# A retention chunk as one step, and the first down stage of a fused RetNet and SwiGLU kernel laid out anew

## The chip, the cores and the metric

The kernel runs on one core of a Trainium2 chip. The metric is the device time of one execution in microseconds (us), the median of three runs. The core's engines are TensorE (PE, matmuls; PEld is its weight load), VectorE (DVE), ScalarE (ACT), GpSimd (POOL) and SyncE (SP), which here only issues DMAs. Each engine has a queue of its own; ACT also issues the stores of the output.

## The reference

A retention layer (a linear recurrence with a decay for each head) is followed by a SwiGLU feed-forward block:

```python
batch, n_heads, seq, head_dim = (4, 8, 768, 64)       # q, k, v
n_tokens, d_model, d_ff = (3072, 512, 1536)           # the block behind it

gamma = 1.0 - 2.0 ** (-5.0 - np.arange(H, dtype=np.float32))
for t in range(S):
    state = gamma[None, :, None, None] * state + np.einsum('bhd,bhe->bhde', k[:, :, t], v[:, :, t])
    y[:, :, t] = scale * np.einsum('bhd,bhde->bhe', q[:, :, t], state)

g = x @ w_gate                       # x: y as (3072, 512)
silu = g * (1.0 / (1.0 + np.exp(-g)))
val = x @ w_val
return (silu * val @ w_out).astype(np.float32)
```

## The kernel before

All arithmetic is fp32. The 3072 tokens are worked through in four segments (s = 0 to 3), each of two halves of three blocks of 128 tokens. A segment has an **up stage** (x by gate and value weights, giving hT) and a **down stage** (hT by w_out). While the down stage of segment s runs, the retention of segment s+1 is done beside it.

Big products use a Strassen scheme in Winograd's form: 7 block products in place of 8, paid for with additions of operands on DVE. The first segment's up stage uses one level. The later ones (`up2`) use two levels: 21 *units* of weights, each of 7 sub-products. A unit's four inner blocks lie in DRAM (`unit_b`, written in the first segment). The three sums that make it whole are done once on DVE (`sums_u`), and the finished unit is stored (`unit_t`), so that the later segments only load it. Some units are summed in the first down stage (`to_sum`), the rest inside the second segment's up stage, two stages ahead of their use. A unit is loaded to one of six ring buffers of which the first four serve the sums in the first down stage.

```python
def load_unit(n, whole, slot=None):
    t = ring[n % RING if slot is None else slot]
    ...
    if whole:
        nc.sync.dma_start(out=t, in_=unit_t[n])                 # 896 KB
    else:
        nc.sync.dma_start(out=t[:, :, ds(U11, 4)], in_=unit_b[n // 7][:, SLOT[PRODUCTS[n % 7]]])

def sums_u(n, engine=nc.vector):                                # three steps
    ...                       # L170: 128x512; L174 and L178: 128x256
    def last():
        sub(w[:, :, U4], w[:, :, U21], w[:, :, U2], op=ALU.subtract)
        nc.sync.dma_start(out=unit_t[n], in_=w)
```

Retention works by chunks of 128 tokens. A chunk has three parts on PE, with tiles of other shapes than the big products: scores (L385, 64x128 tiles; DVE multiplies the result by the decay mask, L391), y (`mix`: L442 with 64x64 and L446 with 128x64 tiles; ACT copies it to xT) and the state (L424, 128x64; DVE adds it, L429). Before:

```python
def retention(s):
    cs = seg_chunks(s)                       # six chunks

    def first(n):
        scores(cs[n]); scale_k(cs[n]); scale_q(cs[n])

    def last(n):
        decay(cs[n]); state(cs[n])
        del chunks[cs[n]]
        if n + 3 < len(cs):
            load_chunk(cs[n + 3], places_of(n))

    steps = [lambda: first(0)]
    for n, c in enumerate(cs):
        if n + 1 < len(cs):
            steps.append(lambda n=n: first(n + 1))
        steps.append(lambda c=c: mix(c))
        steps.append(lambda n=n: last(n))
        if n % 2:
            steps.append(lambda n=n: sums_x(n // 2))
    return steps
```

The down stage handles its three token blocks u = 0, 1, 2 with seven products each (6 matmul steps of 128x256, two passes each in fp32, so 12 in the profile). `step()` is called after each product and puts other work there. `more` makes the next block's operand sums (`sum_h`), `second` is the product B21 and its addition (L727):

```python
if u == 0:
    first(0, range(2, FH)); first(1)
    if s == 0:
        sums_d(0); sum_h(1, 0); second(0); do("t4")      # t4, t5: two last states
        sum_h(2, 0); sums_d(1); second(1); do("t5")      # of the first segment
        sum_h(4, 0); sum_h(3, 0); sums_d(2)
elif u == 2:
    first(u)
product(wb, T1, cur[1]);  nc.scalar.copy(p5, wb);               step()
product(x, T2, cur[2], start=False);  nc.scalar.copy(u2, x);    step()
product(wb, B22, cur[4], start=False)
tt(ev[0][:, DH:], wb, u2, op=ALU.add);  more(1, 2, 4);          step()   # L768
product(x, T3, cur[3], start=False)
tt(ev[1][:, DH:], x, p5, op=ALU.add);  more(3);                 step()   # L772
if s or u == 2:
    second(u)
product(x, T4, a_dn(1, 1, u), start=False)
nc.scalar.copy(ev[1][:, :DH], x)                                         # L778
for i in range(2):
    nc.scalar.dma_start(out=out[ds(row, P)], in_=ev[i]);                 # L782
step()
```

In `up2`, a stage takes 7 time units (one unit is a sub-product of 4 matmuls), and every operation has its time in the list:

```python
at(base, product, x, U11, a[:, 0, 0], True)         # +2 U1, +4 U2, +6 U22, +8 U3, +10 U21, +12 U4
if old is None:
    at(base + 0.5, copy, c11, x);   at(base + 2.5, copy, c22, wb)        # ACT
    at(base + 4.5, copy, c12, x);   at(base + 12.5, copy, c21, x)
...
elif p == 3:   by_block(15.8, 14.3, lambda r: tt(h0[:, r], h0[:, r], p1[:, r], op=mul))   # L663
...
if n + RING < NU:
    at(base + 13.2, load_unit, n + RING, n + RING in prepared)
m = n + 2
if m < NU and m not in prepared:
    for when, k in ((2.2, 0), (4.8, 1), (6.8, 2)):
        at(base + when, lambda k=k: sums_u(m)[k]())
```

The main loop sets what is loaded, summed and stepped beside a down stage:

```python
resident = list(range(RING - 2))
to_sum = list(range(RING - 1, NU, 2)) + resident         # 5, 7, ... 19, then 0 to 3
...
steps = retention(s + 1) + [lambda ps=ps: sums_2(*ps) for ps in ((5, 6), (1, 2), (7,))]

def step():
    k = count[0] = count[0] + 1
    retain((k > 2) + (4 < k < 13) if s else (k > 5) + (7 < k < 18))      # so many steps
    ...
    if count[1] < len(to_sum) and count[1] * 15 < (k - 5) * len(to_sum):
        n = to_sum[count[1]]
        load_unit(n, False, n if n in resident else count[1] % (RING - 2))
        sums.extend(sums_u(n))
        count[1] += 1
    while sums and count[2] * 15 < (k - 6) * 3 * len(to_sum):
        sums.pop(0)()
        count[2] += 1

for u in range(L):
    down(s, u, step)
for st in steps + sums:
    st()
if nxt:
    sums_2(3); sums_2(4)
```

Of the kernel before, what the change touches and what calls it, by code (L numbers as in the profile page):

```python
# [16 lines left out]
P = 128  # L17
# [7 lines left out]
L = 3  # L25
# [16 lines left out]
def tile_retnet_swiglu(  # L42
# [336 lines left out]
    def scores(c):  # L379
        kt, qt = (pairs(t) for t in chunks[c][:2])  # L380
        sp = [bank("s") for i in range(2)]
        for n in range(NP):
            for i in range(2):
                r = ds(D * i, D)
                nc.tensor.matmul(sp[i][:, ts(n, P)], kt[r, n], qt[r, n],  # L385
                                 start=True, stop=True, skip_group_check=True)
        a = []
        for i in range(2):
            j = turn["a"] = turn.get("a", -1) + 1
            t = pairs((iop if c in first_chunks else midp)[:, ts(j % 4, 512)])  # L390
            nc.vector.tensor_tensor(t, pairs(sp[i]), mask[:, i], op=ALU.mult)  # L391
            a.append(t)
        att[c] = a


    def scale_q(c, engine=nc.gpsimd):
        if c % NCK:
            qt = pairs(chunks[c][1])
            engine.tensor_tensor(qt, qt, qdec, op=ALU.mult)

    def scale_k(c, engine=nc.gpsimd):
        if c % NCK < NCK - 1:
# [50 lines left out]
    def retention(s):  # L453

        cs = seg_chunks(s)

        def first(n):
            scores(cs[n])  # L460
            scale_k(cs[n])
            scale_q(cs[n])

        def last(n):
            decay(cs[n])
            state(cs[n])
            del chunks[cs[n]]
            if n + 3 < len(cs):
                load_chunk(cs[n + 3], places_of(n))

        steps = [lambda: first(0)]
        for n, c in enumerate(cs):
            if n + 1 < len(cs):
                steps.append(lambda n=n: first(n + 1))
            steps.append(lambda c=c: mix(c))
            steps.append(lambda n=n: last(n))
            if n % 2:
                steps.append(lambda n=n: sums_x(n // 2))
        return steps

# [219 lines left out]
    def down(s, u, step):  # L700


        x = banks[(u or 0) % 2][:, :DH]

        def product(o, slot, a, start=True):
            for k in range(FH):
                nc.tensor.matmul(o, a[:, k], wot[k][:, slot], start=(start and k == 0),  # L707
                                 stop=(k == FH - 1), skip_group_check=True)

        def tmp(i):  # L710
            return iop[:, ts(8 + i, DH)]

        def first(u, ks=range(FH)):
            o = banks[u % 2][:, :DH]
            for k in ks:
                nc.tensor.matmul(o, a_dn(0, 0, u)[:, k], wot[k][:, B11], start=(k == 0),  # L716
                                 stop=(k == FH - 1), skip_group_check=True)
# [12 lines left out]
        def more(*ns):  # L730
            for n in ns:
                if u + 1 < L:
                    sum_h(n, u + 1)

        if u is None:
            return first
        ev = [iop[:, ts(2 * (u % 2) + i, DM)] for i in range(2)]
        tt = nc.vector.tensor_tensor
        if u == 0:
            first(0, range(2, FH))  # L740
            first(1)
            if s == 0:

                sums_d(0)
                sum_h(1, 0)
                second(0)
                do("t4")
                sum_h(2, 0)
                sums_d(1)
                second(1)  # L750
                do("t5")
                sum_h(4, 0)
                sum_h(3, 0)
                sums_d(2)
        elif u == 2:
            first(u)
        cur = dict(hs)
        wb = bank("wz")[:, :DH]
        product(wb, T1, cur[1])
        p5 = tmp(2)  # L760
        nc.scalar.copy(p5, wb)
        step()
        product(x, T2, cur[2], start=False)
        u2 = tmp(3)
        nc.scalar.copy(u2, x)
        step()
        product(wb, B22, cur[4], start=False)
        tt(ev[0][:, DH:], wb, u2, op=ALU.add)  # L768
        more(1, 2, 4)
        step()  # L770
        product(x, T3, cur[3], start=False)
        tt(ev[1][:, DH:], x, p5, op=ALU.add)  # L772
        more(3)
        step()
        if s or u == 2:
            second(u)
        product(x, T4, a_dn(1, 1, u), start=False)
        nc.scalar.copy(ev[1][:, :DH], x)  # L778
        p, pos = divmod(s * L, NCK)
        for i in range(2):  # L780
            row = (2 * p + i) * S + (pos + u) * P
            nc.scalar.dma_start(out=out[ds(row, P)], in_=ev[i])  # L782
        step()


    kept_vk = consts.tile([P, 2, 512], F32, name="kept_vk")
# [42 lines left out]
        g4 s5 S0 g5 x1 m4 a1 q5 C0 U T0 b1 m5 x2 U D D  # L829
    """)  # L830

    def retain(k):
        for _ in range(k):
            if steps:
                steps.pop(0)()

    for f in range(NF - 1):
        up(f)
# [9 lines left out]

    resident = list(range(RING - 2))
    to_sum = list(range(RING - 1, NU, 2)) + resident
    prepared = set(to_sum)

    for s in range(NSEG):
        nxt = seg_chunks(s + 1) if s + 1 < NSEG else []
        if s == 0:
            for i in range(3):
                load_chunk(nxt[i], places_of(i))
        else:  # L860

            ends = [(7 * n + 13.4, lambda i=i: load_chunk(nxt[i], places_of(i)))
                    for i, n in ((0, NU - 5), (2, NU - 4), (1, NU - 3)) if nxt]


            def begin(s=s):
                down(s, None, None)(0, range(2))

            ends.append((7 * (NU - 1) + 11, begin))
            for n in range(RING - 2, RING):  # L870
                ends.append((-1, lambda n=n: load_unit(n, n in prepared)))
            up2(s, prepared, ends)
            prepared = set(range(NU))
        if s:
            for n in (1, 2, 4, 3):
                sum_h(n, 0)
        steps = []
        if nxt:
            att.clear()
            steps = retention(s + 1) + [lambda ps=ps: sums_2(*ps)  # L880
                                        for ps in ((5, 6), (1, 2), (7,))]
        count, sums = [0, 0, 0], []

        def step():

            k = count[0] = count[0] + 1
            retain((k > 2) + (4 < k < 13) if s else (k > 5) + (7 < k < 18))
            if not nxt:
                return
            if s:  # L890
                if k > 7 and k % 2 == 0 and k // 2 - 4 < RING - 2:
                    load_unit(k // 2 - 4, True)
                return
            if count[1] < len(to_sum) and count[1] * 15 < (k - 5) * len(to_sum):
                n = to_sum[count[1]]
                load_unit(n, False, n if n in resident else count[1] % (RING - 2))
                sums.extend(sums_u(n))
                count[1] += 1
            while sums and count[2] * 15 < (k - 6) * 3 * len(to_sum):
                sums.pop(0)()  # L900
                count[2] += 1

        for u in range(L):
            down(s, u, step)
        for st in steps + sums:
            st()
        if nxt:
            sums_2(3)
            sums_2(4)

# [48 lines left out]
```

## Time and profile before

| | us |
|---|---|
| time, median of 3 (lowest, highest) | 733.93 (733.56, 733.95) |
| span of the profiled execution | 732.1 |
| PE busy | 713.2 (97%) |
| DVE busy | 469.3 (64%) |
| ACT busy | 239.7 (33%) |
| POOL busy | 237.4 (32%) |

The granted TensorE clock is 1.00 throughout. By PE's timeline the first segment's retention runs to 29.3 us, its up stage to 146.5, the first down stage to 225.9; then the up stage of the second segment to 327.5, its down stage to 403.4, the third's to 501.0 and 577.6, the fourth's to 674.8 and the end. A line of the waits names the engine that waited and who released it. The timelines give start, duration and work; a block of several like instructions is one row. A row's duration on PE has the tail of its last matmul in it, so what a block costs is read from start to start.

### The profile page before, as it was taken

The numbers are of one execution on the slowest core, as the hardware profiler recorded it, in microseconds if no ns is written. First come the engines' busy times: TensorE is split into PE (matmuls) and PEld (weight loads), VectorE is DVE, ScalarE is ACT, GpSimd is POOL, SyncE is SP. The second block draws the span as 40 slices with busy tenths as digits, with TensorE's granted clock in tenths as the row PEclk, the third lists the DMA queues.
The fourth block names the chain that finished last, engine by engine and source line by source line (L and its number), as shares of the span: only waits on it lengthen the run. The fifth ranks groups of instructions, "written<-read, shape, count | busy, mean of one in ns | idle before, by whom it ended". The sixth has DMA issues, their size and how long they took to land.

```text
span 732.1 us, 11713 instructions
## 1 busy us (share of the span) xinstructions
PE 713.2 (97%) x4544; PEld 615.4 (84%) x4544; DVE 469.3 (64%) x836; ACT 239.7 (33%) x484; POOL 237.4 (32%) x147
## 2 busy tenths in 40 slices
PE   8898999999999999999999999999999999999997
PEld 7654555687789999998888999998888999999886
DVE  3888998676867888786355465657536356667420
ACT  2668777401212332421121333332121233233000
POOL 1333444512100728380300264363220063726000
PEclk9999999999999999999999999999999999999999
DMA  9797986705989767652642455560373065540010
GB/s 322 254 375 250 288 276 221 271 1 174 381 309 373 278 234 261 220 208 78 207 162 88 135 199 205 200 219 16 108 281 130 29 204 203 200 149 1 1 58 30
DMA packets 60824, 139.06 MB, mean 190 GB/s; under 512 B 4576, under 2 KB 27616, under 8 KB 60768
## 3 DMA queue, kind: packets, MB, share of 16 engines
q1 hardware_dynamic: 57312, 132.01, 52.5%
q10 hardware_dynamic: 3456, 6.29, 2.3%
q8 instruction: 36, 0.59, 0.3%
q14 instruction: 20, 0.16, 0.1%
HBM read 101.72 MB, written 36.57 MB: 189 GB/s over the span
## 4 chain that ended last, share of the span: by engine, by line
PE 85%; DVE 5%; DMA 3%; issue 2%; ACT 1%; SPq 0%; ACTq 0%; DVEq 0%
PE bank L624 37%; PE bank L707 24%; PE bank L513 13%; PE bank L716 4%; PE bank L385 3%; PE bank L446 2%; PE bank L442 2%; DMA ring<-unitb 2%; DMA hsp<-in_w_gate_dram 1%; PE bank L424 1%; DVE ring L170 0%; DVE iop L589 0%; DVE ring L289 0%; DVE midp L391 0%; DVE ring L178 0%
## 5 line engine op out<-in xcount | busy, mean ns | idle before, releaser
L624 PE MATMUL bank<-loadp,ring 128*128 128x192 f32 x720 | 140.6, 327 | 3.1 <-ACT midp L589 2.5
L707 PE MATMUL bank<-wot,hsp 128*128 128x256 f32 x576 | 131.7, 383 | 0.0
L624 PEld LDWEIGHTS bank<-loadp,ring 128*128 128x128 f32 x720 | 120.4, 190 | 4.8 <-ACT midp L589 3.6
L707 PEld LDWEIGHTS bank<-wot,hsp 128*128 128x128 f32 x576 | 107.5, 190 | 16.6 <-issue 1.0
L589 DVE TENSOR_TENSOR iop<-bank,iop 128x384 f32<-128x384 f32 x144 | 79.7, 555 | 56.2 <-PE bank L624 53.2
L624 PE MATMUL bank<-xs,ring 128*128 128x192 f32 x432 | 87.8, 326 | 0.0
L659 POOL TENSOR_TENSOR hT<-iop 128x768 f32<-128x768 f32 x36 | 66.5, 1847 | 36.7 <-DVE iop L589 36.7
L589 ACT COPY hsp<-bank 128x384 f32<-128x384 f32 x90 | 42.9, 479 | 100.4 <-PE bank L624 89.7
L589 POOL TENSOR_TENSOR iop<-hsp,midp 128x768 f32<-128x768 f32 x9 | 16.3, 1814 | 181.5 <-ACT hsp L589 181.5
L624 PEld LDWEIGHTS bank<-xs,ring 128*128 128x128 f32 x432 | 73.2, 190 | 0.0
L707 PE MATMUL bank<-wot,hT 128*128 128x256 f32 x288 | 66.2, 383 | 2.5 <-DVE iop L772 2.5
L624 PE MATMUL bank<-xT,ring 128*128 128x192 f32 x324 | 66.2, 327 | 1.1 <-DVE iop L589 1.1
L513 PE MATMUL bank<-xs,ring 128*128 128x384 f32 x192 | 64.7, 488 | 2.4 <-DVE xs L496 1.7
L707 PEld LDWEIGHTS bank<-wot,hT 128*128 128x128 f32 x288 | 53.8, 190 | 10.8 <-DVE iop L772 2.8
L513 PEld LDWEIGHTS bank<-xs,ring 128*128 128x128 f32 x192 | 36.1, 190 | 29.2 <-issue 2.3
L624 PE MATMUL bank<-hsp,ring 128*128 128x192 f32 x288 | 56.8, 327 | 0.0
L624 PEld LDWEIGHTS bank<-xT,ring 128*128 128x128 f32 x324 | 54.8, 190 | 2.3 <-DVE iop L589 2.2
L589 DVE TENSOR_TENSOR midp<-bank,midp 128x384 f32<-128x384 f32 x72 | 39.9, 555 | 22.8 <-PE bank L624 21.2
L513 PE MATMUL bank<-xT,ring 128*128 128x384 f32 x144 | 49.6, 488 | 1.6 <-DVE hT L550 1.6
L624 PEld LDWEIGHTS bank<-hsp,ring 128*128 128x128 f32 x288 | 48.3, 190 | 0.6 <-ACT hsp L589 0.6
L513 PEld LDWEIGHTS bank<-xT,ring 128*128 128x128 f32 x144 | 27.0, 190 | 21.3 <-DVE hT L550 2.2
L449 ACT COPY xT<-bank 128x512 f32<-128x512 f32 x24 | 14.1, 589 | 89.8 <-PE bank L446 89.8
(146 smaller groups left out, 966.3 us busy)
## 6 DMA issues: line engine op xcount, KB each, us to landing
ring<-unitt SPq DMA_DIRECT2D x50, 896.0 KB, 4.6
unitt<-ring SPq DMA_DIRECT2D x21, 896.0 KB, 4.7
unitb<-ring SPq DMA_DIRECT2D x12, 896.0 KB, 7.7
ring<-unitb SPq DMA_DIRECT2D x21, 512.0 KB, 6.4
out_dram<-iop ACTq DMA_DIRECT2D x24, 256.0 KB, 3.5
loadp<-in_w_val_dram SPq DMA_DIRECT2D x18, 256.0 KB, 3.9
loadp<-in_w_gate_dram SPq DMA_DIRECT2D x9, 512.0 KB, 6.4
midp<-in_w_out_dram SPq DMA_DIRECT2D x12, 256.0 KB, 6.1
```

The source lines that it names most:

```text
L385: nc.tensor.matmul(sp[i][:, ts(n, P)], kt[r, n], qt[r, n], start=True, stop=True, skip_group_check=True)
L424: nc.tensor.matmul(st[ds(D * i, D), n], kd[:, h], vn[:, h], start=(n == 0), stop=True, skip_group_check=True)
L442: nc.tensor.matmul(y[r, ts(n, P)], prev[r, n], qd[r, n], start=(n == 0), stop=False, skip_group_check=True)
L446: nc.tensor.matmul(y[ds(D * i, D), ts(n, P)], vn[:, ts(2 * n + i, D)], a[i][:, n], start=(ci == 0 and n == 0), stop=True, skip_group_check ...
L449: nc.scalar.copy(xT[:, :, c // NCK % 2, ts(ci % L, P)], pairs(y))
L513: nc.tensor.matmul(o, w[:, slot, k], a[:, k], start=(start and k == 0), stop=(stop and k == KH - 1), skip_group_check=True)
L589: events.append((t, len(events), lambda: fn(*args, **kw)))
L624: nc.tensor.matmul(o[:, h], w[:, h, slot], rhs, start=(start and h == 0), stop=True, skip_group_check=True)
L659: by_block(9.5, 13.5, lambda r: pool(to[:, r], u2[:, r], p5[:, r], op=add))
L707: nc.tensor.matmul(o, a[:, k], wot[k][:, slot], start=(start and k == 0), stop=(k == FH - 1), skip_group_check=True)
L716: nc.tensor.matmul(o, a_dn(0, 0, u)[:, k], wot[k][:, B11], start=(k == 0), stop=(k == FH - 1), skip_group_check=True)
```

## The change

Three things are changed together. First, a chunk's scores (of the next chunk), y and state become one step, so that they stand together in PE's order; when a step comes due is written down in a table (`DUE`). Second, which units are summed in the first down stage is chosen by the load that the second segment's up stage has on DVE: what is left to sum there falls to the stages of the products 5, 6, 2 and 7, and not to those of 1, 3 and 4. Third, in the first down stage the products are ordered anew, the unit loads begin at the second step, and the store of a down stage's last block is put off into the next up stage.

```diff
         cs = seg_chunks(s)
-        def first(n): ...          # (cut: scores, scale_k, scale_q)
-        def last(n): ...           # (cut: decay, state, load_chunk)
-        steps = [lambda: first(0)]
-        ...                        # (cut: the loop shown above)
+        def chunk(n):
             if n + 1 < len(cs):
+                scores(cs[n + 1])
+            if n >= 0:
+                mix(cs[n])
+                decay(cs[n])
+                state(cs[n])
+                del chunks[cs[n]]
+                if n + 3 < len(cs):
+                    load_chunk(cs[n + 3], places_of(n))
+            if n + 1 < len(cs):
+                scale_k(cs[n + 1])
+                scale_q(cs[n + 1])
+
+        steps = []
+        for n in range(-1, len(cs)):
+            steps.append(lambda n=n: chunk(n))
+            if n == 5:
+                steps.append(lambda: sums_2(1, 2))
+            if n > 0 and n % 2:
                 steps.append(lambda n=n: sums_x(n // 2))
@@ down
-                do("t4")
+                do("t4 t5")
                 sum_h(2, 0)
                 sums_d(1)
-                second(1)
-                do("t5")
                 sum_h(4, 0)
                 sum_h(3, 0)
                 sums_d(2)
-        elif u == 2:
+        elif u == 2 and s:
             first(u)
@@
         if s or u == 2:
             second(u)
+        else:
+            (second, first)[u](u + 1)
         product(x, T4, a_dn(1, 1, u), start=False)
         nc.scalar.copy(ev[1][:, :DH], x)
-        for i in range(2): ...     # (cut: the two stores, now in store())
+        if u < L - 1 or s == NSEG - 1:
+            store()
         step()
+        return store
@@ main loop
+    DUE = [(5, 7, 9, 10, 11, 13, 14, 15, 17, 18, 19, 20),
+           (3, 5, 7, 8, 9, 11, 12, 13, 15, 16, 18, 20)]
-    resident = list(range(RING - 2))
-    to_sum = list(range(RING - 1, NU, 2)) + resident
+    resident = [0, 1, 2]
+    to_sum = [n for n in range(RING, NU) if n % 7 in (0, 1, 2, 6)][1:] + resident
@@ before up2
+            ends.append((5, store))
@@ step
-            steps = retention(s + 1) + [lambda ps=ps: sums_2(*ps)
-                                        for ps in ((5, 6), (1, 2), (7,))]
+            steps = retention(s + 1) + [lambda: sums_2(5, 6)]
-            retain((k > 2) + (4 < k < 13) if s else (k > 5) + (7 < k < 18))
             if s:
+                if k in DUE[1]:
+                    steps.pop(0)()
...
-            if count[1] < len(to_sum) and count[1] * 15 < (k - 5) * len(to_sum):
-                n = to_sum[count[1]]
-                load_unit(n, False, n if n in resident else count[1] % (RING - 2))
-                sums.extend(sums_u(n))
+            if count[1] < len(to_sum) + 1 and k > 1 and count[1] < 3 + count[2] // 3:
+                n = (to_sum + [3])[count[1]]
+                load_unit(n, False, count[1] % (RING - 2))
+                if n in prepared:
+                    sums.extend(sums_u(n))
                 count[1] += 1
-            while sums and count[2] * 15 < (k - 6) * 3 * len(to_sum):
+            if k in DUE[0]:
+                steps.pop(0)()
+            while sums and count[2] * 12.5 < (k - 6) * 3 * len(to_sum):
...
-        for st in steps + sums:
+        for st in sums:
             st()
         if nxt:
+            sums_2(7)
             sums_2(3)
             sums_2(4)
```

The list is now 7, 8, 9, 13, 14, 15, 16, 20, then 0, 1, 2; unit 3 is loaded in the first down stage but summed in the up stage.

More of the change, by code (lines that the diff above doesn't have):

```diff
@@ L457, in retention @@
         cs = seg_chunks(s)
[L459 to L469, printed above, removed]
-        steps = [lambda: first(0)]
-        for n, c in enumerate(cs):
-            if n + 1 < len(cs):
[L474 to L477, printed above, removed]
+        def chunk(n):
+            if n + 1 < len(cs):
+                scores(cs[n + 1])
[15 more added lines that the diff above has]
+            if n > 0 and n % 2:
                 steps.append(lambda n=n: sums_x(n // 2))
@@ L779, in down, with store @@
         p, pos = divmod(s * L, NCK)
-        for i in range(2):
-            row = (2 * p + i) * S + (pos + u) * P
-            nc.scalar.dma_start(out=out[ds(row, P)], in_=ev[i])
+        def store():
+            for i in range(2):
+                row = (2 * p + i) * S + (pos + u) * P
+                nc.scalar.dma_start(out=out[ds(row, P)], in_=ev[i])
+        if u < L - 1 or s == NSEG - 1:
+            store()
         step()
+        return store
     kept_vk = consts.tile([P, 2, 512], F32, name="kept_vk")
@@ L830, in tile_retnet_swiglu @@
     """)
[L832 to L835, printed above, removed]
+    DUE = [(5, 7, 9, 10, 11, 13, 14, 15, 17, 18, 19, 20),
+           (3, 5, 7, 8, 9, 11, 12, 13, 15, 16, 18, 20)]
     for f in range(NF - 1):
@@ L903, in tile_retnet_swiglu @@
         for u in range(L):
-            down(s, u, step)
-        for st in steps + sums:
+            store = down(s, u, step)
+        for st in sums:
             st()
         if nxt:
+            sums_2(7)
             sums_2(3)
```

## The prediction

> **What bounds the kernel now.** I read the page's busy shares first. TensorE (PE) is busy 97% of the span, and 85% of the chain that ended last is PE. The time can fall only where PE waits, or where its own work becomes cheaper. Next come windows by stage: columns are the stretch, its length, then busy time of PE, weight load, VectorE (DVE), ScalarE (ACT) and GpSimd (POOL), each with its count, then clock, DMA share and GB/s. The rows are the first down stage, the up stage of the second segment, the second down stage and the up stage of the third.
>
> ```profile
> 146.50:225.90 79.40, 76.83 (x625) 64.00 (x626) 58.59 (x113) 11.28 (x33) 11.81 (x9) 1.00 0.61 227
> 225.90:327.50 101.60, 98.13 (x594) 96.06 (x593) 81.43 (x142) 33.95 (x66) 54.15 (x30) 1.00 0.74 262
> 327.50:403.40 75.90, 75.90 (x601) 63.66 (x600) 39.50 (x73) 12.94 (x36) 9.42 (x8) 1.00 0.38 129
> 403.40:501.00 97.60, 97.03 (x594) 96.26 (x593) 59.54 (x104) 34.24 (x66) 49.55 (x28) 1.00 0.54 180
> ```
>
> PE idles 2.6 us in the first row, 3.5 in the second, 0.0 in the third and 0.6 in the fourth. The first two stages are the ones that the change lays out anew. The other PE waits of the list shown next (8.4 of 15.2 us) are before 146.5 us, where the diff touches nothing. Third, the PE waits (total, times, longest):
>
> ```profile
> PE bank L707 <- DVE iop L772: 2.5, 2, 1.8
> PE bank L624 <- ACT midp L589: 2.5, 4, 1.3
> PE bank L624 <- DVE iop L589: 1.8, 3, 0.7
> ```
>
> Nearly all of these 6.8 us lie in the two stages concerned. The PE timeline (start, duration, work; in brackets the idle time before it) says where:
>
> ```profile
> 173.41 2.86 PE L707 MATMUL bank<-wot,hT 128*128 128x256 f32 x12 [1.77 <-DVE iop L772]
> 228.11 1.57 PE L624 MATMUL bank<-loadp,ring 128*128 128x192 f32 x8 [0.76 <-ACT midp L589]
> 240.11 1.57 PE L624 MATMUL bank<-loadp,ring 128*128 128x192 f32 x8 [0.69 <-DVE iop L589]
> 262.10 0.92 PE L624 MATMUL bank<-loadp,ring 128*128 128x192 f32 x4 [1.31 <-ACT midp L589]
> ```
>
> For the first of these, DVE's own timeline shows what stood before L772:
>
> ```profile
> 171.43 0.68 DVE L170 TENSOR_TENSOR ring<-ring 128x512 f32<-128x512 f32 x1
> 172.14 0.42 DVE L178 TENSOR_TENSOR ring<-ring 128x256 f32<-128x256 f32 x1
> 172.59 0.42 DVE L174 TENSOR_TENSOR ring<-ring 128x256 f32<-128x256 f32 x1
> 172.94 0.42 DVE L772 TENSOR_TENSOR iop<-bank,iop 128x256 f32<-128x256 f32 x1
> ```
>
> T4's product adds into the bank that L772 has to empty first. L772 is the fourth of a row behind three sums of a unit (L170, L178, L174), and behind masks before those. It starts at 172.94, while the product T3 that it reads was over by 169.06. The wait is one of DVE's queue, not of DVE's throughput: DVE is busy 58.6 of 79.4 us there.
>
> The wait at 228.11 is explained by ACT's timeline. The two output DMAs take ACT's queue from 226.34 to 227.48, ahead of the two copies that PE needs:
>
> ```profile
> 226.09 0.37 ACT L778 COPY iop<-bank 128x256 f32<-128x256 f32 x1 [9.99 <-PE bank L707]
> 226.34 1.14 ACTq L782 DMA_DIRECT2D out_dram<-iop  x2
> 227.58 0.86 ACT L589 COPY midp<-bank 128x384 f32<-128x384 f32 x2 [1.12 <-PE bank L624]
> ```
>
> Last, what PE itself pays. In the second down stage there are no waits, yet a retention step costs more than its matmuls:
>
> ```profile
> 379.74 1.09 PE L442 MATMUL bank<-ring,state 64*64 64x128 f32 x16
> 380.76 1.09 PE L446 MATMUL bank<-midp,ring 128*64 128x128 f32 x16
> 381.78 2.86 PE L707 MATMUL bank<-wot,hT 128*128 128x256 f32 x12
> 384.57 0.69 PE L424 MATMUL bank<-ring 128*64 128x64 f32 x16
> 385.19 2.86 PE L716 MATMUL bank<-wot,hT 128*128 128x256 f32 x12
> 387.88 10.52 PE L707 MATMUL bank<-wot,hsp 128*128 128x256 f32 x48
> ```
>
> From start to start: a wide product of 12 matmuls takes 2.59 us after a wide one (10.36 / 4 between 387.88 and 398.24, where the next row starts), but 2.79 after a small one (381.78 to 384.57). So a return to the full tile costs 0.20. The state's 16 matmuls (L424) cost 0.62 alone (384.57 to 385.19). Directly behind y they cost 0.47: the same view has y with state behind it at 342.26 and the next product at 343.75, that is 1.49, less the 1.02 of y alone (380.76 to 381.78).
>
> **What the Trainium skill says.** "TensorEngine Tiling (Array Packing)", Key Properties: changing the tiling mode, not just the tile, drains TensorE. The trace agrees in sign and gives the size, 0.20 us per return to 128x128. "TensorE: Matmul & The Clock Gate", in the part on the array being 16 small ones: ACT and DVE are strict first-in-first-out queues. The trace agrees: L772 waits behind sums that it does not need, and ACT's copy behind two DMA issues. "SBUF — State Buffer", "SBUF: two separate sides": the port pair of DVE and GpSimd is an exclusive lock, held for a whole instruction, so that the other one blocks. The trace agrees: a sum L170 takes 0.68 us beside an idle POOL and 1.53 to 1.82 where a POOL addition of 1.81 to 2.15 us overlaps it.
>
> **The change part by part.**
>
> (a) The first down stage's order. Before, u=0 had both "second" products ahead of T1, and for u=0 and u=1 T4 came straight after T3 and a retention step. Now second(1), first(2) and second(2) lie between T3 and T4 of u=0, 1 and 2. The order of PE's instructions confirms it. L772 gets 2.6 us of cover more. For u=0 the three unit sums and more(3) are now queued behind L772 too. For u=1 I let DVE run on from the end of B22 (t): L768 0.4, three sums of h at 0.95 is 2.85, three unit sums 1.5, so L772 ends near t+5.2. PE runs T3 2.6, a chunk's step 3.6, first(2) 2.8, so T4 starts near t+9. For u=2 it is L768 0.4, four sums_2 at 0.47, some 1.2 of unit sums, L772 near t+4, against T3 and second(2), t+5.4. Both waits of L707 on L772 should go: **-2.5 us**.
>
> T1 now comes 2.8 us earlier. It needs sums_d(0), which ends at 150.08, and sum_h(1), which ends at 150.95. PE gets there at about 151.9 + 0.62 + 0.5 = 153.0. T2 at 155.6 needs sum_h(2) (about 154.4) and the first of sums_d(1) (154.7). No new wait, with about 1 us to spare.
>
> (b) One step for a chunk. Counting in PE's order the places where small matmuls are followed by wide ones in the three down stages: 13, 12 and 11 before, 8, 7 and 7 after. That is 14 returns fewer at 0.20, 2.8 us. State blocks that stand directly behind a wide product: 4, 3 and 2 before, 1 after; 8 at 0.15 is 1.2 us. Nothing else of PE's count changes (1289 rows in both). Together **-4.0 us**: about 1.4 in the first stage, 1.5 in the second, 1.1 in the third. All of it is on the path, since PE sets the end there.
>
> (c) Loads of units begin at step 2 instead of 6, sums stay at step 7, and a load runs three units ahead. All 33 sums are then out by step 19; before, sums of the last units ran to 228.1 and held up the queue that issues loads, so that the load of unit 4 was issued at 228.62. It was then summed late: the wait of 0.69 at 240.11 (hole from 239.26, so 0.85 with the restart). Now units 4 and 5 are issued some 6 us earlier, with less traffic beside them (418 GB/s in 226 to 230).
>
> (d) Units to sum inside the up stage: 4, 6, 8 up to 20 before, i.e. one in every other stage. After: 3-6, 10-12, 17-19, one more in all, summed in the stages of products 5, 6, 2 and 7 only. The wait at 262.10 (hole of 1.48 with the restart) ended on an ACT copy behind L663, which DVE did late in the stage of product 4, where it also had unit 8's sums. Those stages are now free of sums.
>
> (e) The store of a down stage's last block moves from its end into the next up stage, behind its first three copies. Hole at 228.11: 226.54 + 0.65 = 227.19, so 0.92. The same place in the third and fourth segment: 404.72 to 405.08 and 578.91 to 579.27, 0.36 each.
>
> (c), (d) and (e) in the second segment: 0.85 + 1.48 + 0.92 = 3.25. Against it I set 0.35 for what DVE may lose (below): **-2.9 us**. In the third and fourth segment: **-0.7 us**. Sum: 2.5 + 4.0 + 2.9 + 0.7 = 10.1 us, 733.93 - 10.1 = **723.8 us**.
>
> **Rivals.** First, DVE becomes the bound in the middle of the up stage. Its load without sums, from 4.55 us windows of the third segment's up stage, is 2.45, 2.16, 2.79, 2.79 us for the second to fifth stage of seven. A unit's sums add 0.68 + 0.42 + 0.42 = 1.5, and up to 1 to 2 more for POOL's lock, as POOL is busy 1.8 to 4.2 us of the third to fifth. That is 4.0, 4.2, 4.8 and 4.8 against 4.55. Four in a row now, where before they alternated. A backlog of half a microsecond fits into the 1.4 us between a tensor_tensor and the matmul that needs it; two microseconds do not. If it goes badly, 1 to 3 us come back, 725 to 727.
>
> Second, the DMA queue. In these stages a store of 0.92 MB and a prepared load of 0.92 MB meet in 4.55 us, 403 GB/s, as much as the busiest windows of before show (418). For it: such windows did delay a sum before (DVE idle 1.38 at 237.5). Against it: loads run six stages ahead. It would cost 1 to 2 us.
>
> Third, the chunk step blocks DVE: the addition of the state waits for matmuls that start only after scores and y, about 2.5 us, and everything behind it waits too. In the first down stage this could push L772 past its cover and bring back one wait of 1 to 2 us. The margins in (a), 1.4 us at the least, speak against it. Fourth, the gain may be larger: the second segment's up stage is 100.8 us from its first to its last matmul (225.89 to 326.68), the third's 96.8 (403.42 to 500.18), 4.0 apart, where I count 3.25 less 0.36. Were all of it gone, the time would be near 722.4.
>
> **Range and chances.** The returns are counted and their price measured, so (b) is firm to half a microsecond. (a) and (e) are likely whole. The doubt is in the up stage, up to 3 us lost or 1 gained. I take 721.5 to 728 as holding 8 times in 10, skewed to the slow side. Faster by over 2% needs 719.3, that is 14.7 us, nearly as much as all waits of PE in the whole run (15.2): 3%. Slower by over 2% would need a new wait in every stage: 2%. Within 2%: 95%.
>
> **What would show it.** The PE waits should have no L772 and no midp copy ended by ACT. PE's timeline should have seven groups of small matmuls in the second and third down stage, with wide pairs of 5.38 us between them. The down stages should last about 75.5, 75.2 and 76.3 us (79.4, 76.7 and 77.4 before, first to last wide product). The second segment's up stage should have PE idle well under 1 us. The prediction is wrong if PE waits for unit sums there, if PE waits at T1 or T2 for sums of h, or if the return to a wide product is no cheaper for being rarer.

## The result, and the profile after

The changed kernel takes **724.08 us** (724.03 to 725.87, 4 runs), the one before 733.74 us in the same measurement (733.44 to 733.95, 4 runs). The ratio is 0.9874, 95% interval 0.9857 to 0.9892. The prediction was 723.8 us, with 721.5 to 728 as its range.

The windows by stage of the changed kernel, with the columns as before (stretch, length, then busy time of PE, weight load, DVE, ACT and POOL):

```profile
146.40:222.40 76.00, 75.43 (x624) 64.46 (x625) 55.70 (x109) 11.22 (x33) 11.98 (x9) 1.00 0.66 244
222.40:320.70 98.30, 97.42 (x594) 96.12 (x593) 80.16 (x145) 34.29 (x66) 54.17 (x30) 1.00 0.75 260
320.70:395.20 74.50, 74.50 (x601) 64.18 (x601) 37.75 (x63) 12.79 (x37) 10.18 (x8) 1.00 0.39 131
395.20:492.50 97.30, 96.92 (x594) 96.19 (x594) 62.00 (x115) 34.21 (x66) 49.55 (x28) 1.00 0.53 180
```

PE idles 0.6 us in the first down stage (2.6 before), 0.9 in the second segment's up stage (3.5 before), nothing in the second down stage, 0.4 in the third segment's up stage. The waits of PE (total, times, longest), those behind 146.4 us:

```profile
PE bank L424 <- issue: 0.8, 2, 0.6
PE bank L626 <- DVE iop L591: 0.7, 2, 0.4
PE bank L626 <- ACT hsp L591: 0.5, 1, 0.5
```

L772 and the copies to midp are gone from the list. New are 0.57 us of "issue" at the state t5 (the other one is in the first segment) and a wait for one of ACT's copies. The two on DVE are at the ends of up stages, where there were two before as well.

The PE timeline of the second down stage shows the chunk step (start, duration, work):

```profile
368.11 1.16 PE L385 MATMUL bank<-ring 64*128 64x128 f32 x16
369.20 1.09 PE L442 MATMUL bank<-loadp,state 64*64 64x128 f32 x16
370.22 1.09 PE L446 MATMUL bank<-midp,loadp 128*64 128x128 f32 x16
371.14 0.64 PE L424 MATMUL bank<-loadp 128*64 128x64 f32 x16
371.71 2.86 PE L709 MATMUL bank<-wot,hT 128*128 128x256 f32 x12
374.40 2.75 PE L718 MATMUL bank<-wot,hT 128*128 128x256 f32 x12
377.08 1.09 PE L442 MATMUL bank<-ring,state 64*64 64x128 f32 x16
```

Scores, y and state stand together, 371.71 - 368.11 = 3.60 us. Then come two wide products in 377.08 - 371.71 = 5.37 us, 0.19 above 2 x 2.59. Before, each product between small matmuls paid 0.20 of its own.

From here on a **stage's length** is read from PE's timeline, from start to start. The first down stage begins behind PE's wait of 0.3 us near 146.4, an up stage with its first 128x192 matmul, and the next down stage with the last sub-product of that up stage (four matmuls of the down stage already stand ahead of it). This is sharper than whole times: a stage that an edit leaves alone repeats within 0.02 us in these profiles (one for each kernel), while the runs of one kernel lie up to 4.2 us apart (725.85 to 730.08 in old_units). So what is under 1 us rests on stage lengths. The stretch up to the first down stage, which no kernel here changes, varies from 145.9 to 147.7 us between profiles, and the whole times vary with it. A **restart** is the part of a hole in PE's work that goes beyond the wait that the profile gives, about 0.16 us.

| | before | after | difference | predicted |
|---|---|---|---|---|
| up to the first down stage | 146.53 | 146.39 | -0.14 | 0 |
| first down stage | 79.36 | 76.03 | -3.33 | -3.9 |
| up stage, second segment | 100.79 | 97.52 | -3.27 | -2.9 |
| second down stage | 76.74 | 75.30 | -1.44 | -1.5 |
| up stage, third segment | 96.76 | 96.50 | -0.26 | -0.36 |
| third down stage | 77.43 | 76.34 | -1.09 | -1.1 |
| up stage, fourth segment | 96.27 | 95.99 | -0.28 | -0.36 |
| sum | | | -9.81 | -10.1 |

The spans differ by 732.1 - 722.3 = 9.8 us, so the table holds the whole change.

### The profile page after: what moved, and what is told of

The parts are those of the page before. It is cut to its first block, busy times and chain, and to the rows that moved or that the text cites. A ratio compares the mean times of both kernels' runs of the same rounds, so it can differ in the third digit from the quotient of the medians.

```text
span 722.3 us, 11724 instructions
## 1 busy us (share of the span) xinstructions
PE 707.4 (98%) x4544; PEld 616.0 (85%) x4544; DVE 467.1 (65%) x836; ACT 239.8 (33%) x484; POOL 239.0 (33%) x147
## 4 chain that ended last, share of the span: by engine, by line
PE 91%; DVE 1%; DMA 1%; ACT 1%; issue 1%; DVEq 0%; ACTq 0%
PE bank L626 40%; PE bank L709 26%; PE bank L515 13%; PE bank L718 4%; PE bank L385 3%; PE bank L446 3%; PE bank L442 2%; PE bank L424 1%; DMA hsp<-in_w_gate_dram 1%; DVE ring L289 0%; DVE iop L591 0%; ACT bank L246 0%; DVE hT L665 0%; ACT loadp L249 0%; DVE ring L261 0%
## 5 line engine op out<-in xcount | busy, mean ns | idle before, releaser
L709 PE MATMUL bank<-wot,hsp 128*128 128x256 f32 x576 | 129.8, 382 | 0.0
L591 DVE TENSOR_TENSOR iop<-bank,iop 128x384 f32<-128x384 f32 x144 | 79.7, 556 | 56.3 <-PE bank L626 52.9
L591 ACT COPY hsp<-bank 128x384 f32<-128x384 f32 x90 | 42.9, 478 | 100.3 <-PE bank L626 89.6
L591 POOL TENSOR_TENSOR iop<-hsp,midp 128x768 f32<-128x768 f32 x9 | 16.3, 1814 | 165.7 <-ACT hsp L591 137.2
L626 PEld LDWEIGHTS bank<-xT,ring 128*128 128x128 f32 x324 | 54.8, 190 | 2.0 <-DVE iop L591 1.8
L591 DVE TENSOR_TENSOR midp<-bank,midp 128x384 f32<-128x384 f32 x72 | 39.8, 554 | 13.8 <-PE bank L626 12.4
L768 DVE TENSOR_TENSOR iop<-bank,iop 128x256 f32<-128x256 f32 x12 | 5.1, 424 | 65.1 <-PE bank L709 48.1
```

Source lines behind the costliest of these rows:

```text
L591: events.append((t, len(events), lambda: fn(*args, **kw)))
L626: nc.tensor.matmul(o[:, h], w[:, h, slot], rhs, start=(start and h == 0), stop=True, skip_group_check=True)
```

## The experiments

All start from the changed kernel. The first five undo or stretch one part of it, the next four go after what it left, the last two combine.

### state_apart: the price of a change of tile

```diff
+        def last(n): decay(cs[n]); state(cs[n]); ...      # out of chunk() for s > 1
+            if n >= 0 and s > 1:
+                steps.append(lambda n=n: last(n))
@@ DUE, and the loop in step() that takes several steps at once
-           (3, 5, 7, 8, 9, 11, 12, 13, 15, 16, 18, 20)]
+           (3, 5, 6, 7, 8, 8, 9, 10, 11, 12, 12, 13, 14, 15, 16, 16, 18, 20)]
```

> The changed kernel, but in the second and third down stage a chunk's state is a step of its own, one product behind y; DVE, DMA and the products are as in the changed kernel. Theory (returns to the full tile cost 0.20 us each, a state alone 0.15 more): 6 states in the second stage and 4 in the third stand apart, so 10 x 0.35 = 3.5 us; the second down stage goes from 75.3 to 77.4 us, the third from 76.3 to 77.7, the time from 724.1 to about 727.6. Rival (the gain of the one step came from waits elsewhere, not from TensorE's own order): both stages stay within 0.3 us and the time at 724.

Measured: second down stage 77.38 us instead of 75.30, third 77.73 instead of 76.34, all other stages unchanged within 0.02; 728.15 us, ratio to before 0.9915 (0.9889 to 0.9942). That is 2.08 + 1.39 = 3.47 us for ten states set apart, 0.347 each. Its PE timeline:

```profile
345.07 2.86 PE L715 MATMUL bank<-wot,hT 128*128 128x256 f32 x12
347.86 0.69 PE L424 MATMUL bank<-loadp 128*64 128x64 f32 x16
348.47 2.86 PE L715 MATMUL bank<-wot,hsp 128*128 128x256 f32 x12
```

The product before the state takes 347.86 - 345.07 = 2.79, the state 0.61: the two prices of the prediction. PE waits for nobody in these stages (no wait is listed there), so the rival falls: the gain of the one step is TensorE's own.

### old_order: the products of the first down stage

```diff
-                do("t4 t5")
+                do("t4")
                 sum_h(2, 0)
                 sums_d(1)
+                second(1)
+                do("t5")
@@
-        elif u == 2 and s:
+        elif u == 2:
@@
-        else:
-            (second, first)[u](u + 1)
```

> The changed kernel with the products of the first down stage in the order of before (second(1) ahead of T1, first(2) at the head of u=2, nothing between T3 and T4 for u=0 and 1). Theory (the products between T3 and T4 cover L772): waits of PE on L772 (here by its new line number) of 1.5 to 2.5 us return, less 0.6 us for the second state t5, which no longer follows t4 directly; first down stage 77 to 78 us instead of 76.0, time 725 to 726. Rival (the earlier loads alone had already freed DVE's queue): no wait on it, stage 75.5 us, time 723.5.

Measured: first down stage 77.96 us (76.03), a wait of 2.10 us on L774 (L772 by its line in this kernel), no "issue" at t5; 727.53 us, ratio 0.9906 (0.9878 to 0.9934). Its DVE timeline shows the old row again: two sums of h (L697), masks and a state, three unit sums, and only then the addition that T4 waits for.

```profile
166.91 1.91 DVE L697 TENSOR_TENSOR hsp<-hsp,hT 128x768 f32<-128x768 f32 x1
168.85 1.68 DVE L697 TENSOR_TENSOR hsp<-hT,hsp 128x768 f32<-128x768 f32 x1
...
171.98 0.68 DVE L170 TENSOR_TENSOR ring<-ring 128x512 f32<-128x512 f32 x1
172.69 0.43 DVE L178 TENSOR_TENSOR ring<-ring 128x256 f32<-128x256 f32 x1
173.15 0.42 DVE L174 TENSOR_TENSOR ring<-ring 128x256 f32<-128x256 f32 x1
173.50 0.41 DVE L774 TENSOR_TENSOR iop<-bank,iop 128x256 f32<-128x256 f32 x1
```

So the earlier loads alone do not free it: it is a matter of the queue's order. The two sums of h take 1.7 us more than the usual 2 x 0.95, while POOL scales q and k (166.69 to 169.71); the three unit sums behind them take 1.5. The kernel before had the same there (1.90 and 1.68). In the changed kernel second(1) no longer takes a step ahead of T1, so the chunk's step falls behind T3 and not ahead of it. L772 then stands ahead of the masks and the unit sums and is over at 166.68, 5.1 us before T4 starts (171.78). The second of the old waits (0.77, u=1) did not return, only one larger one at u=0. The whole time came out above the expected 725 to 726, with the stage where it was expected; the rest is the unchanged head (146.75) and the spread between runs.

### old_units: which units are summed where

```diff
-    resident = [0, 1, 2]
-    to_sum = [n for n in range(RING, NU) if n % 7 in (0, 1, 2, 6)][1:] + resident
+    resident = [0, 1, 2, 3]
+    to_sum = list(range(RING - 1, NU, 2)) + resident
@@ step(): the loads follow this list, without unit 3 as an extra
```

> The changed kernel with the units summed in the first down stage as before (5, 7, ... 19, 0 to 3). Theory (the choice matters because unit 8's sums fall into the stage of product 4): the wait near 36 us into the second segment's up stage returns with 1.3 to 1.5 us, while the early loads keep unit 4 in time; up stage 98.5 to 99 us instead of 97.5, time about 725.4. Rival (that wait came from the late start of the sums, which the new loading mended): up stage at or under 97.5, time 724.

Measured: up stage of the second segment 99.01 us (97.52), a wait of 1.31 us on ACT's copy to midp 34.4 us into it, and 0.70 in place of 0.37 at its end; 726.78 us, ratio 0.9902 (0.9869 to 0.9936). The size of the old wait is met to the hundredth. Its DVE timeline, and then the copy on ACT that PE waits for:

```profile
250.62 1.81 DVE L170 TENSOR_TENSOR ring<-ring 128x512 f32<-128x512 f32 x1
...
253.28 1.10 DVE L178 TENSOR_TENSOR ring<-ring 128x256 f32<-128x256 f32 x1
...
255.56 0.94 DVE L665 TENSOR_TENSOR hT<-hT,midp 128x768 f32<-128x768 f32 x1
```

```profile
256.62 0.48 ACT L591 COPY midp<-bank 128x384 f32<-128x384 f32 x1 [5.46 <-DVE hT L665]
```

Unit 8's first two sums take 1.81 and 1.10 us (0.68 and 0.42 alone) in the stage of product 4, in which DVE also has L665 to do, and L665, which frees p1 for the copy, starts only at 255.56. The choice by DVE's load is worth 1.5 us (the old list also has one unit more in the first down stage, and so one fewer here).

### store_at_end: the DMA issues in ACT's queue

```diff
-        if u < L - 1 or s == NSEG - 1:
-            store()
+        store()
@@
-            ends.append((5, store))
```

> The changed kernel with the store of a down stage's last block at its end. Theory (the two DMA issues stand ahead of the copies in ACT's queue): about 0.3 us return at the head of the third and fourth segment's up stages and 0.4 to 0.9 at the second's; time 725.2 to 725.7. Rival (DVE's addition L729 was late, not ACT): nothing returns, 724.

Measured: up stages 97.83 (97.52), 96.75 (96.50) and 96.26 (95.99) us, so 0.31 + 0.25 + 0.27 = 0.8 us; waits on ACT's copy to midp of 0.27, 0.19 and 0.19; 725.19 us, ratio 0.9875 (0.9846 to 0.9904). The cause is right, and the two later stages are as expected; at the second segment it is 0.31, under the 0.4 to 0.9 expected and far less than the 0.92 that stood there before. The ratio is that of the changed kernel (0.9874), so only the stage lengths and the waits show the effect. In the kernel after, ACT's timeline shows the copies ahead of the issues (ACTq):

```profile
223.96 0.48 ACT L591 COPY midp<-bank 128x384 f32<-128x384 f32 x1 [0.17 <-PE bank L626]
224.80 0.48 ACT L591 COPY midp<-bank 128x384 f32<-128x384 f32 x1 [0.35 <-PE bank L626]
224.86 0.82 ACTq L786 DMA_DIRECT2D out_dram<-iop  x2
```

With the store at the end the issues stand ahead again, and the copy starts 0.10 us behind them (the bracket names another of its waits, which the view takes for the last):

```profile
222.44 0.84 ACTq L786 DMA_DIRECT2D out_dram<-iop  x2
223.38 0.86 ACT L591 COPY midp<-bank 128x384 f32<-128x384 f32 x2 [0.63 <-DVE loadp L580]
```

### late_loads: the pace of loads and sums

```diff
-            if count[1] < len(to_sum) + 1 and k > 1 and count[1] < 3 + count[2] // 3:
+            if count[1] < len(to_sum) + 1 and count[1] * 15 < (k - 5) * (len(to_sum) + 1):
@@
-            while sums and count[2] * 12.5 < (k - 6) * 3 * len(to_sum):
+            while sums and count[2] * 15 < (k - 6) * 3 * len(to_sum):
```

> The changed kernel with the unit loads of the first down stage paced as before (from step 6, spread over 15 steps) and the sums spread over 15 steps too. Theory (early loads get the sums out in time): the last sums run past the end of the stage, the loads of units 4 and 5 are issued after them, and PE waits 0.5 to 1.5 us for a unit or for DVE at the head of the up stage; time 724.7 to 725.6. Rival (the order of the products and the choice of units are enough): no change, 724.

Measured: up stage of the second segment 100.03 us (97.52), waits of 1.28 us (DVE's addition to midp) and 0.69 (an addition behind unit 4's sums) 7.5 and 15.0 us into it; 726.65 us, ratio 0.9889 (0.9872 to 0.9906). The mechanism holds, and it is larger than expected, as two waits come where I had one. The second is the one that the prediction took from the kernel before. The first is DVE's backlog. Its DVE timeline (223.23 is the last unit summed ahead of the stage, 233.72 unit 4):

```profile
223.23 0.68 DVE L170 TENSOR_TENSOR ring<-ring 128x512 f32<-128x512 f32 x1
...
228.35 1.02 DVE L591 TENSOR_TENSOR midp<-bank,midp 128x384 f32<-128x384 f32 x2
...
233.72 2.17 DVE L170 TENSOR_TENSOR ring<-ring 128x512 f32<-128x512 f32 x1 [0.83 <-DMA ring<-unitb]
```

The last unit's sums start at 223.23, the operand sums of x (L580 to L583) follow them without a gap, and only then come the stage's own first two additions (L591), at 228.35, 6.4 us into the stage (it starts at 221.90). In the kernel after, this pair starts at 226.56, 4.1 us into it. PE waits for the second of the pair, which ends at 229.37; its matmul starts at 229.42. The second wait has a late load in it: DVE stands idle for 0.83 us until unit 4 is there, whose load was issued 3.4 us into the stage (225.28), and the sum then takes 2.17 us, beside POOL. So the pace serves two things: the loads, and a DVE that is not behind when the up stage begins. Early loads and quicker sums were undone together here; which of them weighs more was not tried.

### t5_bank: the new wait at t5

```diff
-        st = bank("st")[:, : NP * D]...
+        st = (banks[7] if c == cs0_last else bank("st"))[:, : NP * D]...
```

> The changed kernel with the last state of the first segment (t5) in bank 7 in place of bank 6, which t4 uses. Theory (the 0.57 us of PE before t5, which the profile puts to issue, is t5 waiting until DVE has read t4's result out of the same bank): the wait goes, first down stage 75.4 to 75.5 us instead of 76.0, time 723.5. Rival (t5 waits for its own operands or for issue): the 0.57 stays.

In the kernel after, PE's timeline has t4, a hole, and t5:

```profile
151.76 0.69 PE L424 MATMUL bank<-kept_vk 128*64 128x64 f32 x16
153.02 0.69 PE L424 MATMUL bank<-ring,ring 128*64 128x64 f32 x16 [0.57 <-issue]
153.63 5.45 PE L709 MATMUL bank<-wot,hsp 128*128 128x256 f32 x24
```

DVE reads t4's result in this hole, up to 152.92, and t5 starts 0.10 us later:

```profile
152.50 0.42 DVE L429 TENSOR_TENSOR state<-state,bank 128x256 f32<-128x256 f32 x1
```

With a bank of its own for t5:

```profile
151.45 0.69 PE L425 MATMUL bank<-kept_vk 128*64 128x64 f32 x16
151.97 0.64 PE L425 MATMUL bank<-ring,ring 128*64 128x64 f32 x16
152.53 3.72 PE L710 MATMUL bank<-wot,hsp 128*128 128x256 f32 x16
```

The hole is gone, t5 follows at 0.52 us, and the first down stage takes 75.25 us (76.03): 0.57 of wait and 0.2 of restart. 723.24 us, ratio 0.9845 (0.9825 to 0.9866). So what the profile calls "issue" was the wait for DVE to read t4 out of bank 6.

### unit6_later: the wait on ACT's copy

```diff
-            m = n + 2
+            m = {4: NU, 5: 6}.get(n, n + 2)      # unit 6 in stage 5
```

> The changed kernel with unit 6 summed in stage 5 of the second segment's up stage in place of stage 4. Theory (the 0.52 us of PE at 246.94 is the price of four sums in a row under POOL's lock: DVE late, so ACT's silu late, so its copy late): the wait goes or falls under 0.2 us, time 723.6. Rival (it is only moved): a wait of the same size one stage later, 724.

Measured: the wait of 0.52 is gone, the up stage takes 96.96 us (97.52), but the wait at the stage's end is 0.72 instead of 0.37; 724.16 us, ratio 0.9855 (0.9836 to 0.9874). The stage gains 0.56 net (0.91 ahead of its end, 0.35 lost there). The chain in the kernel after, DVE first, then ACT:

```profile
241.38 1.83 DVE L170 TENSOR_TENSOR ring<-ring 128x512 f32<-128x512 f32 x1
...
244.07 1.10 DVE L178 TENSOR_TENSOR ring<-ring 128x256 f32<-128x256 f32 x1
245.10 0.55 DVE L591 TENSOR_TENSOR midp<-bank,midp 128x384 f32<-128x384 f32 x1
```

```profile
245.68 0.84 ACT L594 ACTIVATE midp<-midp 128x768 f32<-128x768 f32 x1 [3.34 <-DVE midp L591]
246.43 0.84 ACT L591 COPY hsp<-bank 128x384 f32<-128x384 f32 x2
```

L170 of unit 6 takes 1.83 us beside POOL (0.68 alone), L178 1.10 (0.42 alone); the addition to midp ends late, the silu that needs it starts at 245.68, and the copy that PE waits for stands behind the silu in ACT's queue. This is the first rival of the prediction, in its mild form.

### late_mul: the waits at the ends of the up stages

```diff
-                by_block(15.8, 14.3, lambda r: tt(h0[:, r], h0[:, r], p1[:, r], op=mul))
+                by_block(15.8, 15.6 if n == NU - 2 else 14.3, lambda r: tt(...))
```

> The changed kernel with the first half of the last L665 multiplication of an up stage put behind the addition that empties the bank of the last sub-product. Theory (PE's 0.37 us at the end of the second and third segment's up stage, 0.53 with the restart, is DVE's queue, where L665 of 1.44 us, slowed by a POOL scaling, stands ahead of that addition): both go, 0.7 to 1.0 us, time 723.2. Rival (the addition waits for PE itself): nothing changes; or the wait moves to the first sums of h in the down stage.

Measured: both waits are gone and the two up stages are 0.53 and 0.55 us shorter (96.99, 95.95), but the second down stage takes 76.85 us (75.30), with a wait of 1.46 on the sums of h at T1; 724.56 us, ratio 0.9862 (0.9844 to 0.988). The loss was foreseen as a possibility, but not its cause. DVE's timeline of the kernel after at the end of the second segment's up stage, then POOL's; then DVE's and POOL's of this run, where L665 is L666:

```profile
317.98 1.44 DVE L665 TENSOR_TENSOR hT<-hT,midp 128x768 f32<-128x768 f32 x1
319.34 0.55 DVE L591 TENSOR_TENSOR iop<-bank,iop 128x384 f32<-128x384 f32 x1
319.81 1.32 DVE L665 TENSOR_TENSOR hT<-hT,midp 128x768 f32<-128x768 f32 x1
```

```profile
317.56 2.76 POOL L404 TENSOR_TENSOR loadp<-loadp,tab 128x512 f32<-128x512 f32 x2
320.28 1.75 POOL L404 TENSOR_TENSOR ring<-ring,tab 128x512 f32<-128x512 f32 x1
```

```profile
318.43 1.22 DVE L591 TENSOR_TENSOR iop<-bank,iop 128x384 f32<-128x384 f32 x2
319.56 3.50 DVE L666 TENSOR_TENSOR hT<-hT,midp 128x768 f32<-128x768 f32 x2
```

```profile
318.50 2.04 POOL L404 TENSOR_TENSOR loadp<-loadp,tab 128x512 f32<-128x512 f32 x2
320.50 1.75 POOL L404 TENSOR_TENSOR ring<-ring,tab 128x512 f32<-128x512 f32 x1
```

The two multiplications take 3.50 us in a row, where 2 x 0.95 would do. Three scalings of k for the coming chunks (L404), which have nothing to wait for, run ahead on POOL right there, from 318.50 to 322.25. That fits the lock of the port pair that the prediction speaks of; the next run takes the scalings away.

### scale_late: those scalings moved

```diff
-                scale_k(cs[n + 1])
                 scale_q(cs[n + 1])
+                scale_k(cs[n + 1], nc.gpsimd if cs[n + 1] % NCK else nc.vector)
```

> The changed kernel with a chunk's q scaled before its k, and with k scaled by VectorE for the two chunks that begin a batch (they have no scaling of q that would hold POOL back). Theory (three scalings of k run ahead on POOL at the end of the second segment's up stage, one at the end of the third's, and their lock of the port pair stretches L665 from 0.95 to 1.44 and 1.32 us): POOL is idle there, L665 takes 0.95 us, PE's waits at the end of the two up stages fall from 0.37 to under 0.1 and the two stages by 0.3 to 0.5 us each; time 723.2. Rival (DVE's queue is late there for other reasons): the waits stay, and DVE's two scalings of 0.7 us only add to the work in the second down stage; 724 or more.

Measured: the waits at the ends of the up stages are gone, the stages take 97.03 and 95.99 us (97.52, 96.50), the second down stage 75.22; 723.83 us, ratio 0.985 (0.983 to 0.987). DVE's timeline at the same place:

```profile
318.41 0.95 DVE L665 TENSOR_TENSOR hT<-hT,midp 128x768 f32<-128x768 f32 x1
319.27 0.55 DVE L591 TENSOR_TENSOR iop<-bank,iop 128x384 f32<-128x384 f32 x1
319.74 0.95 DVE L665 TENSOR_TENSOR hT<-hT,midp 128x768 f32<-128x768 f32 x1
```

POOL has no work there any more, and L665 takes 0.95. The cause is shown, and the same edit costs the down stage nothing.

### best and best_mul: together

`best` has t5_bank, unit6_later and scale_late; `best_mul` has late_mul as well.

> The changed kernel with t5 in bank 7, unit 6 summed in stage 5 and the scalings as in the run above. If the three parts are independent: 0.78 + 0.56 + about 0.7 us, first down stage 75.25, second segment's up stage 96.6, third's 96.0, time about 722.0. If unit 6's sums and the scalings share one cause (POOL's lock at different places), the parts still add, since they lie in different stretches.

> As the run above, with the last L665 behind the addition as well. Theory (the late multiplication failed before only because three POOL scalings then stood beside both L665): with POOL idle it costs DVE nothing, PE's wait of 1.46 us at the head of the second down stage does not return, and both up stages reach 95.95 to 96.5; time at most 722.0. Rival (the first sums of h have no slack at all): a wait of 0.3 us or more at the head of the second down stage, and no gain over the run above.

Measured: `best` 721.72 us, ratio 0.9821 (0.9802 to 0.9841); first down stage 75.24, up stages 96.12 and 95.99. `best_mul` 721.36 us, ratio 0.9813 (0.9793 to 0.9833); 75.24, 96.08 and 95.95, second down stage 75.16. The parts add in `best`, and the second segment's up stage gains 0.35 us more than the two alone (1.40 against 0.56 + 0.49), as the end wait that had grown to 0.72 is gone too. late_mul no longer harms, as expected, and its own gain over `best` is small: 0.3 us over all the stages, within the spread of the times. The last in time of the PE waits of `best_mul`:

```profile
PE bank L720 <- DVE hT L534: 0.3, 1, 0.3
```

It is the 0.3 at 146.91, the start of its first down stage; behind it PE waits for nobody. By stage lengths `best_mul` is 3.1 us shorter than the changed kernel.

## Why the prediction was right

**(a), the first down stage's order, -2.5.** Right in size: both waits on L772 are gone, and old_order brings one back. T1 and T2 do not wait for sums of h. The mechanism was right only in part. At u=0 it is the place in DVE's queue that counts, L772 ahead of the masks and the unit sums; with 5.1 us to spare, the 2.6 us of cover were not needed. At u=1 old_order has no product between T3 and T4 either, and no wait: the addition stands there behind two unit sums and ahead of the masks, and is over at 196.83, 1.5 us before T4. So the 0.77 of u=1 did not go by the new order of products, and that I counted it there rightly is luck; which other part of the change removed it was not tried. I also put the late L772 of u=0 down to DVE's queue alone, and did not see that two sums of h, longer beside POOL, make up 1.7 us of it by their durations.

The term missed one thing: I let t5 follow t4 in "0.62 + 0.5" us, though both states go through bank 6 and DVE must read the first before the second starts. This cost 0.57 and a restart (0.78 by t5_bank), more than the whole difference between -3.9 and -3.33 in that stage.

**(b), one step for a chunk, -4.0.** Right in size: 1.44 and 1.09 in the stages where it stands alone (1.5 and 1.1), and 0.347 for a state set apart, against 0.35. PE runs 4544 matmuls in both kernels.

**(c), (d), (e), the second segment's up stage, -2.9.** Sum right to 0.4 us (-3.27), allowance included: the unit sums lengthened beside POOL cost a wait of 0.52, where I set 0.35. But the parts are not as I told them, and that their sum fits is partly luck. Undone one at a time they cost 2.51 (loads and sums), 1.49 (units) and 0.31 (store), 4.31 in all, more than they brought together: with the rest of the change in place, each undone part meets others' work. The wait of 1.28 us in late_loads, for one, has no match in the kernel before. Of the 0.92 that I gave to the store, only 0.31 is lost when the store is put back at the end. The two traces show where the rest was. Before, the first of the two issues starts 0.45 us into the stage (226.34), as the store needs L727, which DVE did only at 225.90 to 226.31, although its product was over at 223.30. With the store at the end of the changed kernel that addition is long done, and the first issue starts 0.26 us into the stage. The two issues also took 1.14 us before and 0.84 there. Together, 0.19 and 0.30, that is the difference of the two waits of PE (0.76 and 0.27). So 0.2 us of it was DVE's lateness; why the issues took longer before stays open. The loads of units 4 and 5 were issued 4.0 us earlier relative to the stage (221.15 against a start of 222.42, before 228.62 against 225.89), not the 6 that I had put down, as the last stores still stand ahead of them.

**(e), third and fourth segment, -0.7.** Measured 0.54; store_at_end returns 0.52 of it.

**The rivals.** DVE as the bound came true by half a microsecond only; the DMA queue and the blocked DVE of the chunk step show no wait of PE. The waits at the ends of the up stages, which I left as they were, went from 0.71 and 0.37 to 0.37 and 0.38.

**The sum.** That 9.81 us stand against 10.1 owes something to misses that offset each other: 0.57 too little in the first down stage, 0.37 too much in the second segment's up stage.

## What to carry to other kernels

Where TensorE is busy all the time, count how often it changes its tile shape: grouping small matmuls is worth its price per change (0.20 us here), and that price can be read from two neighbouring rows of the timeline. When an engine with an in-order queue frees a PSUM bank, look at what stands ahead of its work in that queue, and move that behind it; independent products between the matmul that fills the bank and the one that needs it help only where the engine is still late. Work that has no dependency runs early, not late: a scaling on POOL that nothing holds back can fall on the one spot where VectorE has no slack.

## What the runs showed of the hardware that was not expected

A wait for a PSUM bank that VectorE has still to read was listed as "issue" (0.57 us) and went away with another bank. Two 128x768 multiplications on VectorE took 3.50 us beside three GpSimd scalings and 0.95 us each without them. The additions that read PSUM (L591) kept their 0.54 to 0.56 us in the kernel after, beside GpSimd or not.
